# Loading a 4 MB weight as 16 rows and then 112 rows, in a kernel that streams 81 MB through the DMA engines

## Chip, cores, metric

The kernel runs on one core of a Trainium2 chip. The metric is device time in microseconds (us) of one execution; lower is better. "rows" below are rows of 32 KB (16,384 bf16 values), and a row of a weight lands in one of the 128 partitions of SBUF, the on-chip memory. In the tables and profiles PE is TensorE (matrix products), DVE is VectorE, ACT is ScalarE, POOL is GpSimd, and SPq is the queue of SyncE, which issues the loads. The page counts sixteen DMA engines, the units that move the data; a packet is one entry in the record of what they move, here mostly one row.

## The reference, cut to what matters

A gate mixes two branches for four tokens: attention over a window of 4,096 cached keys and values, and a small gated feed-forward block. What matters here is how much has to be read:

```python
W = min(4096, max(256, Sk // 4))                  # 4096
q = (x @ wq)...                                   # wq: 512 x 4096, 4 MB
k = k_cache[:, :, Sk - W:, :]                     # 4 x 8 x 4096 x 128: 32 MB
v = v_cache[:, :, Sk - W:, :]                     # 32 MB
p = softmax(q k^T * Dh**-0.5);  o = p v
a = o @ wo                                        # wo: 4096 x 512, 4 MB
b = ((relu(x @ W_gate)) * (x @ W_up)) @ W_down    # 5.25 MB
out = g * a + (1 - g) * b                         # g = sigmoid(sum(x * gate_w))
```

## The kernel before

All loads are issued by one queue (SyncE) in a fixed order. Query weights, keys and values are loads of 128 rows of 32 KB: 4 MB each, to all 128 partitions. They go into four slots in turn; a load waits only until its slot is free.

```python
def _dma_order():
    o = [("wq",), ("x",), ("gw",), ("k", 0), ("k", 1), ("v", 0)]
    for s in range(2, NSET):
        o += [("k", s), ("v", s - 1)]
    return o + [("wg",), ("wu",), ("v", NSET - 1), ("wd",)] + [("wo", p) for p in range(len(WO_PIECES))]

# on the sync engine, for each of these:
    elif k == "wq":
        load(("WQ",), "d_wq", slot("wq"), A_wq.rearrange("(p t) f -> p (t f)", t=4), waits=w)
    ...   # x, gate_w and the other weights, cut
    else:
        src = (A_k_cache if k == "k" else A_v_cache)[b, 4 * qq:4 * qq + 4, SK - WIN:SK, :]
        load(..., slot(*it), src.rearrange("h (r c) d -> r h (c d)", r=32), waits=w)

# the query product waits for the whole of wq (and for x):
    waits=sc_free(key) + [("WQ",), ("E", "XT"), ("INIT",)]
```

## Time and profile before

| | before |
|---|---|
| median of runs | 196.1 us (196.01 to 196.16) |
| DMA queue's share of 16 engines' span | 97.3% |
| PE / DVE busy | 62% / 64% |
| a 32 KB packet on one DMA engine | 1.214 us (median of 2,176; the prediction has 1.213) |
| query weights landed | 13.15 us |
| last piece of the output weights landed | 192.6 us |

The page of the kernel before (its span is 1.3 us shorter than the device time of the same execution): engine busy times, the DMA share in tenths and the GB/s over 40 slices of the span, and the load queue (packets, MB, share of 16 engines).

```profile
span 194.8 us, 1734 instructions
...
PE 120.6 (62%) x723; PEld 50.6 (26%) x723; DVE 124.1 (64%) x153; ACT 27.5 (14%) x34; POOL 9.5 (5%) x25
...
DMA  6999999999999999999999999999999999999992
GB/s 215 431 432 431 437 437 431 431 427 451 431 437 437 446 427 424 431 437 431 431 431 431 427 424 437 444 437 431 431 431 421 431 395 427 470 431 384 425 404 90
...
q1 hardware_dynamic: 3610, 81.01, 97.3%
```

DMA is at 9 or more from the second slice to the last but one, and the queue's packets take 97.3% of what sixteen engines have. That is the bound: 81 MB at a fixed rate per engine (1.214 us for 32 KB). Nothing else is near it.

The waits of the queue itself (us in all, times, longest):

```profile
SPq L256 <- DVE kt L491: 120.5, 8, 16.4
SPq L256 <- PE bank L320: 38.5, 8, 14.1
```

They look alarming and are not. The view of the DMA issues (count, KB each, median us from issue to landing) says why:

```profile
slots<-in_A_k_cache_dram SPq DMA_DIRECT2D x8, 4096.0 KB, 25.1
...
slots<-in_A_wq_dram SPq DMA_DIRECT2D x1, 4096.0 KB, 12.4
```

A 4 MB key load lands 25.1 us after its issue, while 4 MB take the engines about 9.7 us (eight rows each of 1.214). So two to three loads are always queued, and the DMA engines have work while the queue waits for a slot.

The stretches of the kernel before (us, busy time and instruction count of each engine, granted clock, DMA share, GB/s). A packet counts whole in the stretch in which it starts, so short stretches trade some per cent with their neighbours:

```profile
core 0: us, PE busy (x) PEld busy (x) DVE busy (x) ACT busy (x) POOL busy (x), PEclk, DMA share, GB/s
0.00:5.00 5.00, 0.00 (x0) 0.00 (x0) 3.23 (x2) 1.28 (x1) 3.87 (x13) 1.00 0.65 216
5.00:10.00 5.00, 1.11 (x3) 0.30 (x3) 0.52 (x1) 1.04 (x3) 4.03 (x10) 1.00 1.09 472
10.00:15.00 5.00, 0.76 (x12) 0.51 (x16) 0.17 (x1) 0.84 (x3) 1.62 (x4) 1.00 1.02 440
15.00:20.00 5.00, 4.04 (x40) 1.69 (x32) 2.42 (x10) 1.91 (x2) 0.00 (x0) 1.00 1.02 439
20.00:25.00 5.00, 1.09 (x8) 0.86 (x8) 3.73 (x13) 0.00 (x0) 0.00 (x0) 0.93 0.99 426
25.00:190.00 165.00, 111.53 (x634) 46.19 (x634) 113.61 (x129) 22.09 (x25) 0.00 (x0) 0.90 1.00 429
```

From 5 us on the load runs at its full rate (426 to 472 GB/s in each stretch). The first stretch holds less, because the first packet starts at 1.81 us.

The timeline around the first product: start, duration, engine, what, and what it had waited for.

```profile
13.23 0.27 PE L324 MATMUL bank<-identb,xsb 5*128 5x5 bf16 x4 [5.72 <-DMA xsb<-in_A_x_dram]
...
14.68 3.27 PE L320 MATMUL bank<-slots,xT 128*4 128x512 bf16 x32
...
23.23 4.50 DVE L491 STREAM_TRANSPOSE kt<-slots 128x2048 f32<-128x2048 f32 x2
```

The query product starts at 14.68 us and the first key transpose at 23.23 us.

### The profile page before, as it was taken

The numbers are of one execution on the slowest core, as the hardware profiler recorded it, in microseconds if no ns is written. First come the engines' busy times: TensorE is split into PE (matmuls) and PEld (weight loads), VectorE is DVE, ScalarE is ACT, GpSimd is POOL, SyncE is SP. The second block draws the span as 40 slices with busy tenths as digits, with TensorE's granted clock in tenths as the row PEclk, the third lists the DMA queues.
The fourth block names the chain that finished last, engine by engine and source line by source line (L and its number), as shares of the span: only waits on it lengthen the run. The fifth ranks groups of instructions, "written<-read, shape, count | busy, mean of one in ns | idle before, by whom it ended". The sixth has DMA issues, their size and how long they took to land.

```text
span 194.8 us, 1734 instructions
## 1 busy us (share of the span) xinstructions
PE 120.6 (62%) x723; PEld 50.6 (26%) x723; DVE 124.1 (64%) x153; ACT 27.5 (14%) x34; POOL 9.5 (5%) x25
## 2 busy tenths in 40 slices
PE   0209279474943894686468943894586466743974
PEld 0003123121411341242112411341142122311562
DVE  6103769999399809980998199819981998370010
ACT  2213000040130013001300130013001300420100
POOL 7830000000000000000000000000000000000000
PEclk9999958999999797899876999697999889997899
DMA  6999999999999999999999999999999999999992
GB/s 215 431 432 431 437 437 431 431 427 451 431 437 437 446 427 424 431 437 431 431 431 431 427 424 437 444 437 431 431 431 421 431 395 427 470 431 384 425 404 90
DMA packets 3616, 81.10 MB, mean 416 GB/s; under 512 B 401, under 2 KB 666, under 8 KB 794
## 3 DMA queue, kind: packets, MB, share of 16 engines
q1 hardware_dynamic: 3610, 81.01, 97.3%
q8 instruction: 5, 0.08, 0.2%
q14 instruction: 1, 0.01, 0.0%
HBM read 81.01 MB, written 0.00 MB: 416 GB/s over the span
## 4 chain that ended last, share of the span: by engine, by line
DMA 54%; DVE 31%; PE 9%; issue 4%; SPq 0%; ACT 0%
DMA slots<-in_A_k_cache_dram 38%; DVE kt L491 21%; DMA slots<-in_A_wo_dram 10%; PE bank L320 7%; DMA xsb<-in_A_x_dram 6%; DVE sc L527 5%; DVE qblk L517 1%; PE bank L324 1%; DVE pT L542 1%; DVE rd L531 1%; SPq L256 0%; DVE negmax L537 0%; ACT gwB L600 0%; DVE osum L577 0%; DVE mx L527 0%
## 5 line engine op out<-in xcount | busy, mean ns | idle before, releaser
L491 DVE STREAM_TRANSPOSE kt<-slots 128x2048 f32<-128x2048 f32 x32 | 73.7, 2305 | 28.1 <-DMA slots<-in_A_k_cache_dram 28.0
L320 PE MATMUL bank<-kt,qblk 128*128 128x512 bf16 x256 | 72.1, 434 | 27.9 <-DVE kt L491 27.9
L320 PEld LDWEIGHTS bank<-kt,qblk 128*128 128x128 bf16 x256 | 25.2, 107 | 69.7 <-DVE kt L491 36.0
L320 PE MATMUL bank<-slots,pT 128*64 128x512 bf16 x256 | 32.3, 410 | 5.7 <-DMA slots<-in_A_v_cache_dram 5.7
L619 ACT ACTIVATE pe<-sc,negmax 128x2048 bf16<-128x2048 bf16 x8 | 16.0, 2002 | 60.1 <-DVE negmax L537 60.1
L527 DVE CUSTOM_DVE_ANT_0 sc<-bank,maskf 128x512 bf16<-128x512 f32 x32 | 21.0, 658 | 3.8 <-PE bank L320 3.7
L320 PEld LDWEIGHTS bank<-slots,pT 128*64 128x64 bf16 x256 | 15.1, 118 | 23.2 <-issue 13.4
L542 DVE STREAM_TRANSPOSE pT<-pe 128x2048 bf16<-128x2048 bf16 x8 | 18.5, 2312 | 2.2 <-ACT pe L619 2.2
L604 ACT ACTIVATE osb<-bank 128x512 bf16<-128x512 f32 x8 | 4.8, 597 | 81.5 <-PE bank L320 81.5
L320 PE MATMUL bank<-rd,grpb 128*128 128x32 bf16 x8 | 1.6, 194 | 22.1 <-DVE rd L531 22.1
L555 DVE TENSOR_TENSOR oq<-bank,recip 64x128 bf16<-64x128 f32 x2 | 0.9, 434 | 12.3 <-PE bank L320 12.2
L320 PEld LDWEIGHTS bank<-rd,grpb 128*128 128x128 bf16 x8 | 0.8, 98 | 25.7 <-DVE rd L531 25.7
L495 DVE COPY xT<-bank 128x20 bf16<-128x20 bf16 x1 | 0.2, 171 | 8.0 <-PE bank L324 8.0
L320 PE MATMUL bank<-slots,oq 128*4 128x256 bf16 x64 | 4.0, 272 | 2.0 <-DMA slots<-in_A_wo_dram 2.0
L320 PE MATMUL bank<-slots,xT 128*4 128x512 bf16 (+1 forms) x64 | 5.0, 467 | 0.0
L320 PE MATMUL bank<-maskr,maskl 128*128 128x512 bf16 x1 | 0.6, 609 | 5.9 <-POOL maskr L296 5.9
L517 DVE TENSOR_SCALAR qblk<-bank 32x64 uint32<-32x64 uint32 x16 | 2.9, 215 | 2.1 <-PE bank L324 2.1
L324 PE MATMUL bank<-identb,xsb 5*128 5x5 bf16 x4 | 0.3, 168 | 5.7 <-DMA xsb<-in_A_x_dram 5.7
L577 DVE CAST osum<-bank 4x256 bf16<-4x256 f32 x1 | 0.4, 418 | 5.2 <-PE bank L320 5.2
L320 PEld LDWEIGHTS bank<-slots,oq 128*4 128x4 bf16 x64 | 2.5, 84 | 3.5 <-DMA slots<-in_A_wo_dram 2.9
L296 POOL TENSOR_SCALAR_AFFINE_SELECT fold<-fold 128x256 bf16<-128x256 bf16 x8 | 3.3, 417 | 1.1
L486 DVE MEMSET qblk<- 128x2304 uint32 x1 | 2.0, 1978 | 1.3 <-PEq L644 1.3
(59 smaller groups left out, 40.3 us busy)
## 6 DMA issues: line engine op xcount, KB each, us to landing
slots<-in_A_k_cache_dram SPq DMA_DIRECT2D x8, 4096.0 KB, 25.1
slots<-in_A_v_cache_dram SPq DMA_DIRECT2D x8, 4096.0 KB, 30.5
slots<-in_A_wq_dram SPq DMA_DIRECT2D x1, 4096.0 KB, 12.4
slots<-in_A_wo_dram SPq DMA_DIRECT2D x1, 2176.0 KB, 17.1
slots<-in_B_W_gate_dram SPq DMA_DIRECT2D x1, 1792.0 KB, 19.7
slots<-in_B_W_up_dram SPq DMA_DIRECT2D x1, 1792.0 KB, 23.6
slots<-in_B_W_down_dram SPq DMA_DIRECT2D x1, 1792.0 KB, 18.5
slots<-in_A_wo_dram SPq DMA_DIRECT2D x1, 1152.0 KB, 19.5
```

Source lines behind the costliest of these rows:

```text
L296: op(lambda: e.affine_select(dst, src, pattern, cmp, fill, base=base, channel_multiplier=mult), ev)
L320: E.op(lambda: t.matmul(out_, lhsT, rhs, start=start, stop=stop, tile_position=pos, skip_group_check=True), ev=ev, waits=waits)
L324: E.op(lambda: t.transpose(out_, in_, idn), ev=ev, waits=waits)
L486: E.op(lambda: v.memset(qblk[:, :, :, :, :].rearrange("p s h c e -> p (s h c e)"), 0.0), ev=("QZ",))
L491: E.op(lambda: v.transpose(kt[:, f, :].bitcast(FP32), slot("k", s)[:, 4096 * f:4096 * f + 4096].bitcast(FP32)), ev=("E", "KT", s, f), waits=w)
L517: E.op(lambda dst=dst, r=r, g=g: v.tensor_scalar(dst, src[r, g, 0:B, :, :], 0, None, op0=ALU.bitwise_or), ev=("E",) + keys[1] if (q, g) == ...
L527: E.op(lambda: v.tensor_tensor_reduce(sc[:, 512 * f:512 * f + 512], banks[scb(key)], R["maskf"][:, :], 1.0, -3.0e38, ALU.add, ALU.max, mx4 ...
L531: E.op(lambda: v.tensor_tensor(rd32[:, :, :], bc(R["own8"][:, :].unsqueeze(2), 2, 4), bc(mx4[:, :].unsqueeze(1), 1, 8), ALU.mult), ev=("MA ...
L542: E.op(lambda: v.transpose(pT[:, s % 2, :], pe[:, :]), ev=("E", "PT", s), waits=[("EXP", s)] + ([("PV", s - 2)] if s >= 2 else []))
L555: E.op(lambda g=g, r=r: v.tensor_tensor(oq[r, :, :].rearrange("p i b -> p b i"), banks[tr(key)][0:64, 128 * g:128 * g + 128].rearrange("p ...
L604: E.op(lambda: a.activation(osb[:, s, :], ob(s), ACTF.Copy), ev=("NORM", s), waits=[("PV", s)])
L619: E.op(lambda: a.activation(pe[:, :], sc[:, :], ACTF.Exp, bias=negmax[:, s % 2:s % 2 + 1], scale=SCALE, accum_out=rowsum[:, s:s + 1]), ev= ...
```

## The change

The sixteen first packets of the kernel before do not start together: the first at 1.81 us, the last at 2.77. The change wants every DMA engine to have work at once: it issues 16 rows, as many as there are engines, and then the other 112.

```diff
--- before.py
+++ after.py
@@ -25,6 +25,7 @@
 OUTT = 2
 OW = 512 // OUTT
 OR = 128 // OUTT
+WQ_ROWS = ((0, 16), (16, 128))
 WO_PIECES = ((0, 34), (34, 52), (52, 60), (60, 63), (63, 64))
 LOW3 = (0, 123, 126, 128)
 
@@ -263,7 +264,9 @@
             elif k == "gw":
                 load(("GW",), "d_gw", xsb[4:5, :], gate_w.rearrange("(o p) -> o p", o=1))
             elif k == "wq":
-                load(("WQ",), "d_wq", slot("wq"), A_wq.rearrange("(p t) f -> p (t f)", t=4), waits=w)
+                wq = A_wq.rearrange("(p t) f -> p (t f)", t=4)
+                for n, (lo, hi) in enumerate(WQ_ROWS):
+                    load(("WQ", n), f"d_wq{n}", slot("wq")[lo:hi, :], wq[lo:hi, :], waits=w)
             elif k == "wg":
                 load(("WG",), "d_wg", Wg, B_W_gate.rearrange("(p t) f -> p (t f)", t=4), waits=w)
             elif k == "wu":
@@ -349,7 +352,7 @@
                         c = (4 * n + j) * 512
                         mm(banks[scb(key)][32 * j:32 * j + 4, :], xT[:, 5 * q:5 * q + 4], Wq[:, q, c:c + 512],
                            q == 0, q == 3, ev=key if (q, j) == (3, 3) else None, pos=(0, 32 * j),
-                           waits=sc_free(key) + [("WQ",), ("E", "XT"), ("INIT",)] if (q, j) == (0, 0) else ())
+                           waits=sc_free(key) + [("WQ", 0), ("WQ", 1), ("E", "XT"), ("INIT",)] if (q, j) == (0, 0) else ())
 
         def QT():
             for n in range(2):
```

## The prediction

> **What bounds the kernel now.** The DMA engines. The queue table gives the load queue 97.3% of sixteen engines' span (81 MB, mean 416 GB/s); the slice row shows DMA at 9 from the second slice to the last but one, while DVE is at 64% and PE at 62%. In the packet records a 32 KB row takes an engine 1.213 us (median of 2,176), about 27 GB/s, early and late alike. No slot wait empties the queue: its waits look long (120 us on the key transposes), but a 4 MB load takes about 9.7 us of all engines and key loads land 25 us after issue, so two to three loads are always queued. Hence time = first packet + bytes per engine at a fixed rate + a tail of about 3 us (last landing near 192.2, final sum, store).
>
> **What the change does.** One 128-row issue (0.40 us on the queue engine, first packets 0.6 us after it ends) becomes a 16-row and a 112-row issue.
>
> - Removed: the staggered start. The sixteen first packets start at 1.81 to 2.77 us. [...]one row per engine should start them all by about 1.95. But early starters take 1.9 to 2.3 us for that first row and late ones 1.3 to 1.8: first rows END at 3.75 to 4.33 whatever their start, so most of the stagger is already hidden. I estimate a gain of 0 to 0.3 us.
> - Added: one issue, about 0.4 us, ahead of x, gate_w and the first keys. It is hidden[...]. One more completion write per engine (9 ns). The query matmuls wait for both parts; they start at 14.7, off the critical path.
> - Bytes, rate and the final tail do not change.
>
> **The risk, larger than the gain.** Rows 0 to 15 are partitions 0 to 15. [...] Against it: at 190.4 to 191.0 us[...] 512 B rows (27 ns each)[...] while the laggards' 4 KB packets stay at 159 to 167 ns, as when alone. No collision shows. I hold no port effect at 60%, a partial one at 15%, the full one at 25%.
>
> **Prediction.** 196.0 us, 195.5 to 200.0. Faster by over 2%: 0.01; within 2%: 0.76; slower by over 2%: 0.23.
>
> **What would show it.** Right: first packets all start within 0.2 us of 1.8 and take 1.2 to 2.3 us; the query weights land at 13.0 to 13.4; last output-weight landing at 191.9 to 192.3.[...]
>
> **What would make it wrong.** [...]the 112 rows spread over fewer engines; engines leaving the first loads unevenly[...].

What the sum came to: the 196.1 us of the kernel before, less an estimated gain of 0 to 0.3, is 195.8 to 196.1, put at 196.0. The upper end, 200.0, leaves 3.9 us for a loss by where the rows are written, which the record calls "port effect" and holds at 15% (partial) and 25% (full). The terms of that loss and the signs expected of it are cut where marked, because they rested on figures that no trace of this case shows; so are the reasons given for the earlier start and for the hidden issue, and who moved the 512 B rows at the tail.

## More of the kernel before

No record names the engine that moved a packet.

The key buffer `kt` (32 KB in each of 128 partitions) is written by VectorE for the first time at 23 us; before that it is free, which the experiments use.

## The result, and the profile after

204.91 us (204.58 to 205.42, 4 runs) against 196.06 us: 4.5% slower (ratio 1.0453, 95% interval 1.0433 to 1.0473). A ratio here is the mean time of one kernel's runs over that of the other's of the same rounds, so it is not quite the ratio of the medians quoted. Where a difference in us is given, it is the difference of the two medians.

The page after, with the lines that answer to those above:

```profile
span 204.1 us, 1736 instructions
...
PE 122.6 (60%) x723; PEld 51.8 (25%) x723; DVE 123.9 (61%) x153; ACT 27.5 (13%) x34; POOL 9.5 (5%) x25
...
DMA  8899999999999999999999999999999999999991
GB/s 128 186 302 245 385 456 443 417 417 421 462 430 424 417 432 456 421 417 417 443 462 417 417 414 443 456 424 417 424 437 456 414 401 427 456 449 385 427 390 54
...
q1 hardware_dynamic: 3626, 81.01, 97.1%
```

The DMA engines are as busy as before (8 in the first two slices, 9 in all others but the last, 97.1% of the span), but the first four slices of about 5 us move 128, 186, 302 and 245 GB/s instead of 215, 431, 432 and 431. This is the reading to learn: busy time of a DMA engine is not work done. A packet that takes longer counts as busy all that time (the first sixteen took 3.69 us each, before 1.93). Look at GB/s beside it.

The queue's own waits after:

```profile
SPq L257 <- DVE kt L494: 124.0, 8, 16.5
SPq L257 <- PE bank L327: 23.0, 1, 23.0
SPq L257 <- PE bank L323: 21.2, 7, 6.7
```

They are of much the same size in sum (168 us, before 159), and the loads are still queued well ahead. The issues after:

```profile
slots<-in_A_k_cache_dram SPq DMA_DIRECT2D x8, 4096.0 KB, 25.4
...
slots<-in_A_wq_dram SPq DMA_DIRECT2D x1, 3584.0 KB, 20.9
...
slots<-in_A_wq_dram SPq DMA_DIRECT2D x1, 512.0 KB, 6.7
```

The 112 rows landed 20.9 us after their issue; all 128 took 12.4 before. The key loads have kept their distance: 25.4 us from issue to landing, before 25.1.

The stretches after:

```profile
core 0: us, PE busy (x) PEld busy (x) DVE busy (x) ACT busy (x) POOL busy (x), PEclk, DMA share, GB/s
0.00:5.00 5.00, 0.00 (x0) 0.00 (x0) 3.22 (x2) 1.28 (x1) 3.87 (x13) 1.00 0.78 111
5.00:10.00 5.00, 1.11 (x3) 0.30 (x3) 0.52 (x1) 1.04 (x3) 4.03 (x10) 1.00 0.97 203
10.00:15.00 5.00, 0.00 (x0) 0.00 (x0) 0.00 (x0) 0.00 (x0) 1.62 (x4) 1.00 1.12 315
15.00:20.00 5.00, 0.00 (x0) 0.00 (x0) 0.00 (x0) 0.00 (x0) 0.00 (x0) 1.00 0.87 216
20.00:25.00 5.00, 2.18 (x28) 1.00 (x32) 0.17 (x1) 0.87 (x3) 0.00 (x0) 1.00 1.02 401
25.00:190.00 165.00, 107.99 (x572) 43.09 (x566) 118.70 (x147) 23.36 (x25) 0.00 (x0) 0.89 1.00 430
```

Between 5 and 20 us the kernel moved 203, 315 and 216 GB/s, before 472, 440 and 439; from 25 us on both have 429 or 430. The whole loss lies in the first 23 us, and it is kept from there on. The landings say the same: query weights at 22.15 us (before 13.15, so 9.0 later), first keys at 31.86 (22.84, 9.0 later), last output weights at 201.48 (192.60, 8.9 later).

```profile
21.80 0.27 PE L327 MATMUL bank<-identb,xsb 5*128 5x5 bf16 x4 [14.30 <-DMA xsb<-in_gate_w_dram]
...
23.26 3.38 PE L323 MATMUL bank<-slots,xT 128*4 128x512 bf16 x32
...
31.88 2.31 DVE L494 STREAM_TRANSPOSE kt<-slots 128x2048 f32<-128x2048 f32 x1
```

The query product starts 8.6 us later, and so does the first transpose. That is a consequence: the loads go on without a gap meanwhile (DMA share 1.00 and 430 GB/s from 25 us on), so PE or DVE waiting there costs nothing by itself.

The packet records show where the time goes. Below are the 32 KB packets of each kernel in order of their start, taken in sets of sixteen (as many as there are engines): mean us of each set.

```
set      1     2     3     4     5     6     7     8     9    10    11
before 1.93  1.23  1.21  1.21  1.21  1.21  1.21  1.21  1.21  1.21  1.21
after  3.69  2.83  2.19  1.76  1.86  1.98  2.13  2.09  1.65  1.22  1.22
```

The first eight sets are the query weights, the ninth the first keys. A set of the query weights took 1.5 to 2.3 times as long as the same set before. The stagger that the change was after did shrink: first packets start at 1.80 to 2.14 us. But they end at 4.84 to 6.15 us, before at 3.75 to 4.33.

### The profile page after: what moved, and what is told of

Same layout as the page of the kernel before. It is cut to its first block, busy times and chain, and to the rows that moved or that the text cites. A ratio compares the mean times of both kernels' runs of the same rounds, so it can differ in the third digit from the quotient of the medians.

```text
span 204.1 us, 1736 instructions
## 1 busy us (share of the span) xinstructions
PE 122.6 (60%) x723; PEld 51.8 (25%) x723; DVE 123.9 (61%) x153; ACT 27.5 (13%) x34; POOL 9.5 (5%) x25
## 3 DMA queue, kind: packets, MB, share of 16 engines
q1 hardware_dynamic: 3626, 81.01, 97.1%
## 4 chain that ended last, share of the span: by engine, by line
DMA 67%; DVE 16%; PE 12%; issue 4%; SPq 1%; ACT 0%
DMA slots<-in_A_k_cache_dram 42%; DMA slots<-in_A_v_cache_dram 15%; DVE kt L494 12%; PE bank L323 11%; DMA xsb<-in_gate_w_dram 10%; DVE sc L530 2%; SPq L257 1%; DVE oq L558 0%; ACT gwB L603 0%; DVE rd L534 0%; DVE negmax L540 0%; DVE osum L580 0%; PE bank L327 0%; DVE xT L498 0%; DVE mx L530 0%
## 5 line engine op out<-in xcount | busy, mean ns | idle before, releaser
L323 PE MATMUL bank<-kt,qblk 128*128 128x512 bf16 x256 | 73.5, 441 | 24.0 <-DVE kt L494 24.0
L323 PEld LDWEIGHTS bank<-kt,qblk 128*128 128x128 bf16 x256 | 25.8, 109 | 67.4 <-DVE kt L494 31.7
L323 PE MATMUL bank<-slots,pT 128*64 128x512 bf16 x256 | 33.2, 419 | 5.7 <-DMA slots<-in_A_v_cache_dram 5.7
## 6 DMA issues: line engine op xcount, KB each, us to landing
slots<-in_A_k_cache_dram SPq DMA_DIRECT2D x8, 4096.0 KB, 25.4
slots<-in_A_wq_dram SPq DMA_DIRECT2D x1, 3584.0 KB, 20.9
```

Of the source, the lines that this page charges most:

```text
L323: E.op(lambda: t.matmul(out_, lhsT, rhs, start=start, stop=stop, tile_position=pos, skip_group_check=True), ev=ev, waits=waits)
```

## The experiments

Three theories:

- **Port theory.** The partitions that a load writes set its rate. The name is the record's; no trace shows a port, and only the partitions are varied. The record also has a stricter form, "matching" or "mismatch", in which the order of the rows counts as well.
- **Source theory.** The rows that are read together (next to each other, or seven apart) set the rate.
- **Issue theory.** A second issue, a small load at the cold start, or the sizes 16 and 112 as such cost time.

"e_" runs split the query weights in another way. "d_" runs leave the kernel before as it is and put an additional load of query-weight rows into the unused key buffer ahead of everything; since the kernel is bound by the load, the time added is the price of that load. All gave correct results. The additional load looks like this (here 16 rows). Between d_ runs only the two row ranges differ, except that d_all128 takes the first 4 KB of all rows and d_112src another tensor:

```diff
+                wq = A_wq.rearrange("(p t) f -> p (t f)", t=4)
+                ktf = kt[:, :, :].rearrange("p f c -> p (f c)")
+                load(("DUP",), "d_dup", ktf[0:16, :], wq[0:16, :])
                 load(("WQ",), "d_wq", slot("wq"), ...)
-            w = [("K", s)] + ([("SC", s - 1, f)] if s else [])
+            w = [("K", s)] + ([("SC", s - 1, f)] if s else [("DUP",)])
```

| run | what is loaded | us added |
|---|---|---|
| e_cols | query weights by columns, 4 KB then 28 KB of all rows | +0.08 |
| e_last16 | rows 0 to 111, then 112 to 127 | +9.97 |
| e_half | rows 0 to 63, then 64 to 127 | +10.50 |
| e_evenodd | even rows, then odd rows | +0.14 |
| e_4x32 | every fourth row, four times | +0.23 |
| d_all128 | 512 KB more: 4 KB of 128 rows | +1.18 |
| d_16 | 512 KB more: 16 rows to partitions 0 to 15 | +3.93 |
| d_16dst8 | the same rows to partitions 0, 8, ... 120 | +2.41 |
| d_16src8 | rows 0, 8, ... 120 to partitions 0 to 15 | +4.38 |
| d_32 | 1 MB more: 32 rows to partitions 0 to 31 | +4.97 |
| d_32s4 | the same rows to partitions 0, 4, ... 124 | +2.56 |
| d_64s2 | 2 MB more: 64 rows to partitions 0, 2, ... 126 | +5.27 |
| d_64mid | the same rows to partitions 32 to 95 | +5.10 |
| d_96 | 3 MB more: 96 rows to partitions 32 to 127 | +14.38 |
| d_112 | 3.5 MB more: 112 rows to partitions 16 to 127 | +14.92 |
| d_112src | the same partitions, other source rows | +13.87 |
| d_128 | 4 MB more: 128 rows | +9.89 |

### Is it the second issue? e_cols

```diff
-load(("WQ",), "d_wq", slot("wq"), A_wq...)
+for n, (lo, hi) in enumerate(((0, 2048), (2048, 16384))):
+    load(("WQ", n), f"d_wq{n}", slot("wq")[:, lo:hi], wq[:, lo:hi], waits=w)
```

> Two issues as in the change, but cut by columns: 4 KB of all 128 rows, then 28 KB of all rows. Port theory (destination partitions of a load set its rate) and row-pattern theory (which rows the engines read together): as before, 196.1 us within 0.3. Issue theory (a second issue or a short first load is what costs): about +9 us, 204 to 206.

196.15 us against 196.07 (ratio 1.0, 0.9984 to 1.0017). Two issues with a short first one cost nothing. The issue theory fell in its plain form.

### Is it the cold start? e_last16

The pieces became `((0, 112), (112, 128))`.

> 112 rows first (partitions 0 to 111), then 16 (112 to 127[...]). Port theory: the loss stays, +6 to +10 us, the weights land at 19 to 23 us. A theory that only the very first, cold load suffers from being 16 rows: most of the loss goes away.

206.04 us, +9.97. The loss stays, and is 1.1 us larger than with the small part first. The sixteen rows at the end took 3.67 us a packet, with nothing cold about them.

### What do 16 rows cost by themselves? d_all128 and d_16

> The kernel before with an additional load ahead of all: 512 KB as 128 rows of 4 KB into the still unused key buffer. Every theory: +1.2 to +1.5 us, the price of the bytes at 27 GB/s per engine. It is the yardstick of the next run.

> The same additional 512 KB as 16 rows of 32 KB into partitions 0 to 15. Port theory with the size seen after the change: the first packets take 3.7 us in place of about 2, so +2.9 to +3.5 us in all, about 1.7 to 2 more than the 128-row form. If the 16-row load costs nothing by itself: +1.2.

512 KB cost 1.18 us as 128 short rows and 3.93 us as 16 long ones: 2.75 us more for the same bytes. First two stretches of d_all128, then of d_16:

```profile
0.00:5.00 5.00, 0.00 (x0) 0.00 (x0) 3.23 (x2) 1.28 (x1) 3.88 (x13) 1.00 0.72 256
5.00:10.00 5.00, 1.11 (x3) 0.30 (x3) 0.51 (x1) 1.04 (x3) 4.03 (x10) 1.00 1.05 452
```

```profile
0.00:5.00 5.00, 0.00 (x0) 0.00 (x0) 3.23 (x2) 1.28 (x1) 3.87 (x13) 1.00 0.72 105
5.00:10.00 5.00, 1.10 (x3) 0.30 (x3) 0.52 (x1) 1.04 (x3) 4.03 (x10) 1.00 0.95 315
```

In the first 5 us of d_16 the sixteen rows have begun and nothing else: sixteen times 32 KB in 5 us are those 105 GB/s. The 128-row form has begun more than twice as much. The 16 rows landed at 7.26 us, 5.45 us after their first packet had started. The packet table says why the kernel lost less than that: after 3.59 us for the first set the next set still took 2.28 us and only then came 1.22. So part of the 16 rows' time ran under the next load. The two sets together took 2.71 us more than the first two of the kernel before (1.93 and 1.23), and 2.75 were lost.

### Destination or source? d_16dst8 and d_16src8

```diff
-                load(("DUP",), "d_dup", ktf[0:16, :], wq[0:16, :])
+                load(("DUP",), "d_dup", ktf[0:128:8, :], wq[0:16, :])     # d_16dst8
+                load(("DUP",), "d_dup", ktf[0:16, :], wq[0:128:8, :])     # d_16src8
```

> The additional 16 rows of 32 KB, same source rows 0 to 15, but into partitions 0, 8, ... 120[...]. Port theory: between the yardstick and the 16 adjacent partitions, +1.5 to +2.3 us over before. Source theory[...]: no better than adjacent partitions.

> The additional 16 rows from source rows 0, 8, ... 120 into partitions 0 to 15. Port theory: as the adjacent source rows, +2.9 to +3.5 us. Source theory: better or worse than those by over 0.5 us.

With the source rows kept, every eighth partition in place of 0 to 15 took the price from 3.93 to 2.41 us (I had expected at most 2.3). The strided load also starts later: its issue took 0.61 us against 0.38, and its first packet starts at 2.20 us against 1.80. So the effect of the partitions is, if anything, larger than the difference of the two prices. With the partitions kept, other source rows moved it from 3.93 to 4.38: 0.45 us, under the mark that I had set for a source effect, and both are above the 2.9 to 3.5 that I had expected. The first two stretches of d_16dst8, against those above:

```profile
0.00:5.00 5.00, 0.00 (x0) 0.00 (x0) 3.23 (x2) 1.28 (x1) 3.87 (x13) 1.00 0.78 210
5.00:10.00 5.00, 1.11 (x3) 0.30 (x3) 0.52 (x1) 1.04 (x3) 4.03 (x10) 1.00 0.97 419
```

Two sets of packets have begun in the first 5 us in place of one, and the second stretch is near full rate already.

### What do 112 rows cost? d_112, d_128, d_112src

```diff
+                load(("DUP",), "d_dup", ktf[16:128, :], wq[16:128, :])     # d_112
+                load(("DUP",), "d_dup", ktf[:, :], wq[:, :])               # d_128
+                load(("DUP",), "d_dup", ktf[16:128, :], A_k_cache.rearrange(
+                     "b h (r c) d -> (b h r) (c d)", c=128)[0:560:5, :])    # d_112src
```

> An additional load of 112 rows of 32 KB into partitions 16 to 127, nothing else changed. Bytes alone: +8.5 us. [...]about 6 to 7 us more: +14 to +16.

> An additional load of all 128 rows of 32 KB. Every theory: bytes alone, +9.7 us; packets of 1.21 us. Yardstick of the 112-row run.

128 rows cost 9.89 us, 112 rows 14.92: fewer bytes, 5.0 us more. Seven eighths of 9.89 are 8.65, so the 112 rows lose 6.27 us. Together with the 2.75 of the 16 rows that makes 9.02 us; the change measured +8.85. So the two parts add up to the loss, and the larger part of it is the 112 rows.

> The additional 112 rows into partitions 16 to 127, but read from every fifth 32 KB row of the key cache, so the addresses that engines read together are quite different. Port theory: +14.9 us as with the query weights as source, within 0.7. Source theory: over 1 us away, down to +8.5.

209.99 us, +13.87: 1.05 us below d_112. By the letter of the expectation that is neither: outside the 0.7 allowed to the port theory, barely past the 1 us of the source theory. Read as sizes, about 1 of the 6.3 us follows the source addresses (or the other tensor), and 5.2 us stay when the source changes entirely. So the source has a small effect of its own.

### The same split with other partitions: e_half and e_evenodd

These two have the same number of issues, the same sizes and 64 rows in each part.

```diff
+for n, (lo, hi) in enumerate(((0, 64), (64, 128))):                       # e_half
+    load(("WQ", n), f"d_wq{n}", slot("wq")[lo:hi, :], wq[lo:hi, :], waits=w)
+for n in range(2):                                                        # e_evenodd
+    load(("WQ", n), f"d_wq{n}", slot("wq")[n:128:2, :], wq[n:128:2, :], waits=w)
```

> The query weights as rows 0 to 63, then 64 to 127: same bytes, four rows per engine each[...]. Port theory:[...] +7 to +10 us. A theory that it is the uneven sizes 16 and 112 or the seven rows per engine that cost: about as before, under +2.

> The query weights as even rows, then odd rows: same two issues, sizes and four rows per engine as rows 0 to 63 then 64 to 127[...]. Bare port theory: as before, 196.1 within 0.7.[...] If 64-row loads are slow as such: +10.5, as the halves.

206.62 us (+10.50, a little over the +10 expected) and 196.35 us (+0.14). The first four stretches of e_half, then of e_evenodd:

```profile
0.00:5.00 5.00, 0.00 (x0) 0.00 (x0) 3.23 (x2) 1.28 (x1) 3.88 (x13) 1.00 0.78 170
5.00:10.00 5.00, 1.10 (x3) 0.30 (x3) 0.52 (x1) 1.04 (x3) 4.02 (x10) 1.00 0.99 203
10.00:15.00 5.00, 0.00 (x0) 0.00 (x0) 0.00 (x0) 0.00 (x0) 1.63 (x4) 1.00 1.03 216
15.00:20.00 5.00, 0.00 (x0) 0.00 (x0) 0.00 (x0) 0.00 (x0) 0.00 (x0) 1.00 0.93 190
```

```profile
0.00:5.00 5.00, 0.00 (x0) 0.00 (x0) 3.22 (x2) 1.28 (x1) 3.87 (x13) 1.00 0.59 210
5.00:10.00 5.00, 1.11 (x3) 0.30 (x3) 0.52 (x1) 1.04 (x3) 4.03 (x10) 1.00 0.99 426
10.00:15.00 5.00, 0.61 (x12) 0.50 (x16) 0.17 (x1) 0.69 (x2) 1.62 (x4) 1.00 1.05 453
15.00:20.00 5.00, 4.60 (x40) 1.86 (x32) 1.88 (x7) 1.71 (x3) 0.00 (x0) 1.00 1.08 465
```

From 5 to 15 us e_half moves 203 and 216 GB/s at a DMA share of 0.99 and 1.03; e_evenodd moves 426 and 453 at 0.99 and 1.05. In e_half the packets take 2.56 us, twice 1.214 and 5% more, in e_evenodd 1.21 to 1.23 after the first set. Both run one part after the other, with the same sizes. But this pair changes the source rows of each part together with the partitions, so it does not separate the two; d_32 and d_32s4 below, with the same source rows, do.

### The intent without the fault: e_4x32

`slot("wq")[n:128:4, :]` for n = 0 to 3: the first issue has 32 rows, two for each of sixteen engines, to every fourth partition.

> The intent of the change without its fault: four loads of 32 rows, every fourth row[...], so the first issue gives each engine two rows. Port theory: within 0.5 us of before (the strided issue took 0.6 us, so the start may be 0.2 later); packets 1.21 us. It beats before only if the stagger at the start was worth something: at most -0.3.

196.44 us against 196.21 (ratio 1.0012, 0.9995 to 1.0029). No loss, and no gain either. Its first packets start at 2.13 to 3.09 us, no earlier than before; issuing took 0.62 us each (2.48 us for four) against 0.40 for the 128-row load. So it did not realise the intent. e_cols did: its first packets (4 KB) start at 1.83 to 2.07 us, and it gained nothing (+0.08). I found no version that beats the kernel before.

### Is it where the rows go, and is that all? d_32, d_32s4, d_96, d_64mid, d_64s2

> The same 32 source rows into partitions 0 to 31[...]. Port theory, either form:[...] +4 to +4.9 us. Source theory: as the run with every fourth partition.

> An additional load of 32 rows of 32 KB (1 MB) into partitions 0, 4, ... 124[...]. Bytes alone: +2.4 us.[...] The port theory in its bare form[...] says +2.4; the matching form[...] says +4 to +5.

d_32: +4.97, twice what 1 MB takes at the full rate (2.43 us, two rows of 1.214 for each engine) and 0.11, with packets of 2.56 us after the first set. d_32s4: +2.56, the price of the bytes alone (2.43) and 0.13. The source rows, their number and the single issue are the same; only the partitions differ. This settles it for these loads: where a load goes sets its price. I had also allowed +4 to +5 us for the strided form (the matching form of the theory). That did not come; after the first set, packets took 1.24 us.

> An additional load of 96 rows into partitions 32 to 127[...]. Bytes alone +7.3[...]. Bare port theory: 9.7 to 10.2.[...]

+14.38 us. That is above the 9.7 to 10.2 of the bare form, and 4.5 us above d_128 (+9.89), which moves a third more bytes. The stretches from 5 to 15 us:

```profile
5.00:10.00 5.00, 1.11 (x3) 0.30 (x3) 0.52 (x1) 1.04 (x3) 4.03 (x10) 1.00 1.04 223
10.00:15.00 5.00, 0.00 (x0) 0.00 (x0) 0.00 (x0) 0.00 (x0) 1.62 (x4) 1.00 1.03 223
```

That is close to the 203 and 216 GB/s of e_half. I tried the mismatch again, with the same 64 source rows to two sets of partitions:

> An additional load of 64 rows into partitions 32 to 95[...]. Bare port theory[...]: +4.9 to +5.3 us. Mismatch theory[...]: +7 to +10 us, packets near 2.4 us.

> The same 64 source rows into partitions 0, 2, ... 126[...]. Both theories: +4.9 to +5.3 us, packets of 1.21 us, as the even and odd halves of the weights showed. It is the yardstick of the other.

+5.10 and +5.27: no clear difference, packets of 1.21 to 1.23 us in both after the first set. The mismatch form, which put the first at +7 to +10, failed for the second time. d_64mid says one thing more. Partitions 32 to 95 are adjacent, as 0 to 63 are, and yet run at the full rate, where in each half of e_half a packet took 2.56 us. So it is not adjacency that costs. Why 32 to 95 run at the full rate and 0 to 63 do not is not shown.

**What stays open.** Loads of 112 and 96 rows cost 5.0 and 4.5 us more than the load of all 128 (14.92 and 14.38 against 9.89), and the records do not say which engine wrote which row.

- How the rows are dealt to the engines is not shown. The slowdown is not that of a few engines: in d_96 no row after the first sixteen took under 1.48 us. The median row took 2.36 us in d_96 and 2.13 in d_112; six and seven rows per engine at that pace make 14.2 and 14.9 us (my estimate), which is the whole price.
- A rival is left. Every load of 96 or 112 rows went to a block of partitions, none to a strided set, so the totals do not exclude that these numbers of rows cost by themselves. One thing in the records, found afterwards, speaks against it. Of the seven sets of 112 rows, the third was the fastest with partitions 16 to 127 (1.61 us in d_112, 1.60 with the other source), and the fifth, which is the third from the end, with partitions 0 to 111 (1.65 us in e_last16). The pattern turned round with the partitions, which the number of rows alone would not make it do.

So: the extra cost goes with 96 or 112 rows in a block of partitions, in d_96, d_112 and e_last16. What causes it is not shown.

## Why the prediction was wrong

1. **The bound (right).** The DMA engines bound the kernel, and time lost at their start is not regained: 9.0 us later at the query weights, 8.9 at the last output weights.
2. **The gain (right in size).** The starts drew together from 1.81–2.77 to 1.80–2.14 us (forecast: all by about 1.95). That this is worth next to nothing was right too: e_cols, whose first packets start at 1.83 to 2.07 us and each part of which goes to all 128 partitions, is 0.08 us from before.
3. **The added issue (right).** e_cols and e_evenodd: +0.08 and +0.14 us.
4. **The weight given to the risk (wrong; this step failed).** The prediction named the effect, and it came: the first packets took 3.0 to 4.2 us (mean 3.69), the stretch from 2 to 5 us shows 87 GB/s (before 262), the weights landed at 22.15 us and the final landing came later by as much (8.9 us). But it put "no port effect at 60%", "the full one at 25%". The reason given was one reading: at 190.4 to 191.0 us packets of 512 B (27 ns) and of 4 KB (159 to 167 ns) are in flight together, and "No collision shows". That this tested the effect was an assumption, since no record names an engine or the partitions of a packet. A small, indirect observation at the tail was given a weight that only a direct measurement could have earned; d_16 is such a measurement (+3.93 us, d_all128 +1.18). What the runs showed in place of "no port effect": the same 32 source rows cost 4.97 us into partitions 0 to 31 and 2.56 into every fourth, and the change lost 8.85 us.
5. **The size (wrong).** The range ended at 200.0, 3.9 us above before; measured +8.85. Of that the 16 rows have 2.75 us over the price of the bytes (d_16 less d_all128); part of their time runs under the next load. The 112 rows have 6.27 (d_112 less seven eighths of d_128), more than the whole range allowed. That part was the larger one and the worse known, and why it is so large stays open.

## What to carry to other kernels

Split a load by columns (e_cols, +0.08 us), or by rows with a stride of two or four (e_evenodd +0.14, e_4x32 +0.23); when the load is the bound, not into a block of partitions before you have measured that block. Partitions 0 to 15, 0 to 31 and the halves 0 to 63 and 64 to 127 were slow (3.93 us for 0.5 MB, 4.97 for 1 MB, +10.50 for the two halves); 32 to 95 ran at the full rate (5.10 us for 2 MB). So a block is not bad as such. Blocks of 96 and 112 rows cost more than all 128 (14.38 and 14.92 us against 9.89). Before you cut a transfer, list the partitions of each part, and measure each part as an additional load; the number of rows per engine did not tell the price (32 rows cost 4.97 or 2.56 us). When DMA is busy all the time, read GB/s beside it: at a share of 0.99 the engines moved 203 GB/s in e_half and 426 in e_evenodd.
